# An expert layer's weights used as fp32 instead of as two fp32r halves

## The chip, the cores and the metric

One core of one Trainium2 chip runs the whole kernel in one launch. The metric is device microseconds, the median of several runs. All times come from such runs or from one profiled execution of the kernel before.

## The reference

Three stages follow each other. The change touches the last one alone.

```python
attn = softmax(rmsnorm(q) @ rmsnorm(k).T / 8) @ v          # 4 batches x 12 heads, 448 rows of 64
x = attn as [1792, 768]
# first expert layer: each token goes to its best expert of 8
x[mask] = gate_w[mask, None] * (np.maximum(x[mask] @ w1[e], 0) @ w2[e])
# second expert layer: each expert takes 224 tokens, handed out in order of the highest logit
for idx in np.argsort(-(x @ w_gate).flatten()):
    tok, e = idx // 8, idx % 8
    if assigned[tok] < 0 and counts[e] < 224: assigned[tok] = e; counts[e] += 1
for e in range(8):
    h = np.maximum(x[assigned == e] @ w1[e], 0.0)          # 224x768 @ 768x1024
    out[assigned == e] = h @ w2[e]                         # 224x1024 @ 1024x768
```

All arrays are fp32.

## The kernel before

`moe2` computes the second expert layer. Handing out the tokens is a sequential job: after each phase one more expert is full. The class `Assigner` does it, mostly in short vector instructions (comparisons of bids, lines 1599 to 1960), with small matmuls, transposes and copies on the other engines. Phase 0 is over before `moe2` begins its products; in the path that ran, a compaction follows (line 1913), then phases 1 to 6 (`phase`: `bids`, `count`, `settle`, `put`) and a short `last`. Each ends with `ids` (line 1865), the row numbers of one expert's tokens.

The products of one expert run beside the phases of later ones. For each expert `n` in the order in which they fill up:

- `gather` fetches its 224 token rows in two halves by indirect DMA on the GpSimd queue (L2076); `turn` transposes them (12 transposes, L2084).
- The weights come in 14 pieces on SyncE's queue (L2051): six of w1 (128x1024, 512 KB) and eight of w2 (128x768, 384 KB). They land in a ring of six places (`raws`). `split` makes two fp32r halves of each piece: ScalarE copies the high half (L2066), and VectorE or GpSimd subtracts it for the low half (L2057). The table `ON_V` says which: all six w1 pieces of an expert after the first go to VectorE, all w2 pieces to GpSimd. A fp32 product is then high times high, high times low and low times high.
- The transposed tokens are halved likewise (ScalarE L2088, VectorE L2090).
- First product, 48 steps (8 column blocks `f` by 6 row blocks `k`): `acc` issues three matmuls of 224 columns (L2098 to L2100). `relu` copies on ScalarE (L2123, L2124) and subtracts on GpSimd. When no assignment step is left, `acc2` issues a matmul of 448 and one of 224 columns (L2107, L2108) and `relu2` does a chain on ScalarE and VectorE (L2113 to L2118).
- Second product, 32 steps (2 token halves, 2 column halves, 8 `k`): `gemm2` issues three matmuls of 384 columns (L2135 to L2137). `store` copies out and scatters by indirect DMA (L2142, L2143).

The order on each engine is written out when the program is built. `Pace.work` keeps a clock for each engine with the costs given in the code, such as `work("p", 0.32, t)` for a step of the first product and 0.485 for one of the second; ahead of each step of the experts it emits all assignment steps that would be ready by then. The engines run their queues in order, so a matmul of the assignment that waits for VectorE holds the experts' matmuls behind it on TensorE.

The first weight piece is loaded as soon as expert 0 is known; a memset on GpSimd (behind the gathers on that queue) holds the next ones back until the gathers are issued, and the fourth w1 piece of each later expert likewise (L2047).

Of the kernel before, what the change touches and what calls it, by code (L numbers as in the profile page):

```python
# [1960 lines left out]
def moe2(tc, consts, wt, qkv, x0, asn, w1, w2, y, out):  # L1961
# [8 lines left out]
    with ExitStack() as ctx:  # L1970
# [3 lines left out]
        w1h, w1l, w2h, w2l = wt  # L1974
# [5 lines left out]
        raws = [t[:, FF * i : FF * i + FF] for t in qkv for i in range(3)]  # L1980
        xx = p2.tile([128, KD, 2, CAP], F32R, name="xx")
        xh, xl = xx[:, :, 0, :], xx[:, :, 1, :]
        hh = p2.tile([128, KF, CAP], F32R, name="hh")
        hl = p2.tile([128, KF, CAP], F32R, name="hl")
        zr = x0[0]
        xgs = [p2.tile([CP, YW], F32, name=f"xg{i}") for i in range(2)]
        hrs = [p2.tile([128, CAP], F32, name=f"hr{i}") for i in range(NHR)]

        def product(f):
            return pg2[f % 2][:, : 2 * CAP]  # L1990
# [37 lines left out]
        nload, nsplit = 0, 0  # L2028

        arrival, there, done = {}, {}, {}  # L2030
# [6 lines left out]
        def pump(eng=nc.sync, most=6):  # L2037
            nonlocal nload
            while nload < nsplit + most:
                n, first, k = piece(nload)  # L2040
                if n >= len(regs):
                    break
                if (n, first, k) == (n, True, LATE) and n:

                    if (n, 1) not in fetched:
                        break
                    nc.gpsimd.memset(raws[nload % 6][0:1, 0:1], 0.0)  # L2047
                r, w, wd = raws[nload % 6], w1 if first else w2, FF if first else DM
                clock["d"] = max(clock["d"], clock["p"] + DELAY, choice[n]) + wd * 1.43e-3
                arrival[nload] = clock["d"]  # L2050
                eng.dma_start(out=r[:, :wd], in_=w[bass.ds(regs[n], 1), 128 * k : 128 * (k + 1), :].rearrange("a p f -> p (a f)"))  # L2051
                nload += 1

        def subtract(out, in0, in1, t, width, on_v):

            t = work(*(("v", 0.05 + width * 1.07e-3) if on_v else ("g", width * 2.25e-3)), t)
            (nc.vector if on_v else nc.gpsimd).tensor_tensor(out=out, in0=in0, in1=in1, op=OP.subtract)  # L2057
            return t

        def split(n, first, k):  # L2060
            nonlocal nsplit
            assert piece(nsplit) == (n, first, k) and nload > nsplit
            r = raws[nsplit % 6]
            h, l, wd = (w1h, w1l, FF) if first else (w2h, w2l, DM)
# [3 lines left out]
            nsplit += 1  # L2068
            if nsplit > 1:
                pump()  # L2070
# [31 lines left out]
        def acc2(n, pg, f, k):  # L2102

            fs = slice(128 * f, 128 * f + 128)
            t = max(there[n, True, k], there["x", 0, k // 3], there["x", 1, k // 3])
            done[f] = work("p", 0.285, t)
            nc.tensor.matmul(pg, lhsT=w1h[:, k, fs], rhs=xx[:, k].rearrange("p a c -> p (a c)"), start=k == 0, stop=False)  # L2107
            nc.tensor.matmul(pg[:, :CAP], lhsT=w1l[:, k, fs], rhs=xh[:, k, :], start=False, stop=k == KD - 1)  # L2108

        def relu2(pg, f):  # L2110
            hr = hrs[f % NHR]
            t = work("s", 0.25, max(done[f], there.get(("h", f - NHR), 0.0)))
            nc.scalar.activation(hr, pg[:, CAP:], AF.Copy)  # L2113
            t = work("v", 0.3, t)
            nc.vector.tensor_tensor(out=hr, in0=pg[:, :CAP], in1=hr, op=OP.add)  # L2115
            nc.vector.tensor_scalar(hh[:, f, :], hr, 0.0, None, op0=OP.max)  # L2116
            there["h", f] = work("v", 0.6, t)
            nc.vector.scalar_tensor_tensor(hl[:, f, :], hr, 0.0, hh[:, f, :].bitcast(F32), op0=OP.max, op1=OP.subtract)  # L2118

        def relu(pg, f, on_v=False):  # L2120
            hr = hrs[f % NHR]
            t = work("s", 0.68, max(done[f], there.get(("h", f - NHR), 0.0)))
            nc.scalar.activation(hr, pg, AF.Relu)  # L2123
            nc.scalar.activation(hh[:, f, :], hr, AF.Copy)  # L2124
            there["h", f] = subtract(hl[:, f, :], hr, hh[:, f, :].bitcast(F32), t, CAP, on_v)

        def gemm2(n, h, t):
# [28 lines left out]
        start = nload, nsplit, known, list(regs), dict(asn.__dict__)  # L2156

        def experts(compact):
            nonlocal nload, nsplit, known
            nload, nsplit, known = start[:3]  # L2160
            regs[:] = start[3]
            choice[:] = [0.0]
            fetched.clear()
            asn.__dict__.update(start[4])
            arrival.update((i, 0.0) for i in range(FIRST))
            pace.start(phases(compact), g=2.0, d=3.5)
            ready.update({0: 4.5, 1: 5.5})
            split(0, True, 0)
# [8 lines left out]
            split(0, True, 1)  # L2177
            for n in range(E):
                turns, gathered, turned = [], 0, 0
                splits = iter(range(KD) if n + 1 < E else ())  # L2180
                both = pace.step is None

                def ahead(t):
# [7 lines left out]
                    elif t >= 17:  # L2191
# [8 lines left out]
                        if t % 2 and nload > nsplit and arrival[nsplit] <= clock["p"] + EARLY:  # L2200
                            k = next(splits, None)
                            if k is not None:
                                split(n + 1, True, k)

                for t in range(32):
                    k2 = t // 2 + 2
                    if n and t % 2 == 0 and 2 <= t <= 16:
                        (relu2 if both else relu)(product(t // 2 - 1)[:, : CAP << both], t // 2 - 1)
                    if n == 0 and 7 <= t < 7 + KF:
                        split(0, False, t - 7)  # L2210
                    if t % 2 == 0:
                        if n == 0 and k2 < KD:
                            split(0, True, k2)
                        elif n and k2 < KF:
                            split(n, False, k2)
# [6 lines left out]
                    if t < 16:  # L2222
                        if n:
                            f, a = divmod(t, 2)
                            for k in range(3 * a, 3 * a + 3):
                                (acc2 if both else acc)(n, product(f)[:, : CAP << both], f, k)
# [5 lines left out]
                        elif t < 6 + KF:  # L2232
# [4 lines left out]
                            for i in range(f - 1, f + 1) if f % 2 else ():  # L2237
                                relu(first_product(i), i, i in ON_V[4])
                    else:
                        gemm2(n, (t - 16) // 8, t % 8)  # L2240
                if n + 1 == E:
# [9 lines left out]
                for k in splits:  # L2251
                    split(n + 1, True, k)
                split(n + 1, False, 0)
                split(n + 1, False, 1)
# [13 lines left out]
EARLY = 0.3  # L2268
# [15 lines left out]

ON_V = (0, 1, 3, 5), range(6), (), (), ()


def fused_kernel(tc, q, k, v, g_q, g_k, modality_id, w_gate, bias, w1, w2, w_gate2, w12, w22, out):
    nc = tc.nc
    with ExitStack() as ctx:  # L2290
        cpool = ctx.enter_context(tc.tile_pool(name="cpool", bufs=1))
        dpool = ctx.enter_context(tc.tile_pool(name="dpool", bufs=1, space=bass.MemoryType.DRAM))
        wp1 = ctx.enter_context(tc.tile_pool(name="wp1", bufs=1))
        xp = ctx.enter_context(tc.tile_pool(name="xp", bufs=1))
        xs = dpool.tile([N, DM], F32, name="xs")
# [4 lines left out]
        rp = ctx.enter_context(tc.tile_pool(name="rp", bufs=1))  # L2300
# [42 lines left out]
```

## Time and profile before

| | us |
|---|---|
| median of 3 runs | 1146.68 |
| lowest, highest | 1145.34, 1154.47 |
| the profiled execution | 1148.52 |
| its span, first to last instruction | 1146.5 |
| mean granted TensorE clock in it | 0.932 of full |

The span is what the profile's rows cover; 2.0 us of the profiled execution lie outside it. Attention fills the span to about 350 us, the first expert layer to about 705 us, and `moe2` the rest.

### The profile page before, as it was taken

What the parts mean: (1) busy time and instruction counts of PE and PEld (TensorE: products, weight loads), DVE (VectorE), ACT (ScalarE), POOL (GpSimd) and SP (SyncE); (2) the same over time, 40 slices, a digit from 0 to 9 for tenths busy, and PEclk for the clock granted to TensorE, in tenths of its full rate; (3) what the DMA queues carried; (4) which work ended last, traced back from release to release, by engine and by line L of the source; (5) the groups of instructions that cost most, each with busy time, mean ns of one, the idle gap of its engine ahead of it and who ended that gap; (6) DMA issues with size and microseconds to landing.
All of it is one profiled execution on the core that took longest, in us unless ns stands there. A gap on an engine that the chain in (4) does not pass through costs nothing. (4 is left out here: it accounts for less than half of the span.)

```text
span 1146.5 us, 19734 instructions
## 1 busy us (share of the span) xinstructions
PE 1029.6 (90%) x6480; PEld 823.0 (72%) x6480; DVE 670.0 (58%) x1634; ACT 527.7 (46%) x1139; POOL 384.1 (33%) x330
## 2 busy tenths in 40 slices
PE   7999999999996999999999988588798969889875
PEld 6566555556554888889889876577687869789775
DVE  5777877868857511113212127868888783786670
ACT  3677777677783222224422228342444344355330
POOL 4533344343145110010501010252627162663350
PEclk7999999999998999999999989588797889999988
DMA  6566555555462173466201010515616082675530
GB/s 150 134 155 154 132 142 142 132 138 130 118 190 73 57 263 112 167 235 232 80 30 57 28 49 11 185 61 188 197 40 218 32 250 89 200 235 168 163 108 27
DMA packets 80903, 151.10 MB, mean 132 GB/s; under 512 B 14254, under 2 KB 53422, under 8 KB 80752
## 3 DMA queue, kind: packets, MB, share of 16 engines
q1 hardware_dynamic: 75552, 126.06, 37.8%
q0 software_dynamic: 5200, 23.33, 6.5%
q8 instruction: 58, 0.95, 0.4%
q14 instruction: 93, 0.76, 0.2%
HBM read 110.69 MB, written 17.44 MB: 112 GB/s over the span
## 5 line engine op out<-in xcount | busy, mean ns | idle before, releaser
L205 DVE TENSOR_REDUCE nm<-sp 112x1 f32<-112x448 f32 x192 | 117.9, 619 | 57.3 <-PE sp L204 29.5
L211 ACT ACTIVATE e<-sp,nm 112x448 f32<-112x448 f32 x192 | 121.8, 634 | 54.7 <-DVE nm L205 35.1
L2057 POOL TENSOR_TENSOR w2l<-qkv,w2h 128x768 fp32r<-128x768 f32 x64 | 124.1, 1954 | 59.8 <-ACT w2h L2066 36.6
L219 PE MATMUL tp<-ident,e 112*112 112x112 f32 x768 | 111.8, 269 | 0.6 <-DVE et L222 0.6
L219 PEld LDWEIGHTS tp<-ident,e 112*112 112x112 f32 x768 | 81.7, 135 | 26.1 <-issue 19.0
L232 PE MATMUL op<-et,qkv 112*64 112x448 f32 x384 | 99.4, 565 | 0.0
L225 ACT ACTIVATE et<-tp 112x448 f32<-112x448 f32 x144 | 78.4, 545 | 36.6 <-PE tp L219 35.1
L2135 PE MATMUL bank<-w2h,hh 128*112 128x384 f32 x256 | 91.1, 356 | 0.0
L2137 PE MATMUL bank<-w2h,hl 128*112 128x384 f32 x256 | 86.9, 339 | 0.0
L2136 PE MATMUL bank<-w2l,hh 128*112 128x384 f32 x256 | 86.7, 339 | 0.0
L2107 PE MATMUL bank<-xx,w1h 128*128 128x448 f32 x192 | 67.2, 400 | 21.1 <-DVE hr L2115 21.0
L200 PE MATMUL sp<-bt,at 128*112 128x448 f32 x188 | 85.4, 454 | 0.7 <-DMA bt<-cut 0.6
L908 PE MATMUL po<-w2h,hh 128*128 128x384 f32 x240 | 85.5, 356 | 0.1
L137 POOL TENSOR_TENSOR xn<-qkv,rr 112x512 f32<-112x512 f32 x47 | 48.0, 1053 | 112.2 <-DVE rr L128 112.2
L909 PE MATMUL po<-w2l,hh 128*128 128x384 f32 x240 | 81.5, 339 | 0.5 <-DVEq L837 0.5
L880 PE MATMUL pg<-w1h,xh 128*128 128x512 f32 x180 | 75.0, 417 | 7.1 <-ACTq L1192 5.7
L911 PE MATMUL po<-w2h,hl 128*128 128x384 f32 x240 | 80.2, 339 | 0.0
L984 POOL DMA_INDIRECT y<-yr,ti x11 | 11.5, 1041 | 194.6 <-POOLq L837 165.1
L882 PE MATMUL pg<-w1h,xl 128*128 128x512 f32 x180 | 71.2, 396 | 0.0
L881 PE MATMUL pg<-w1l,xh 128*128 128x512 f32 x180 | 70.8, 393 | 0.0
L2098 PE MATMUL bank<-xx,w1h 128*128 128x224 f32 x192 | 68.4, 356 | 0.0
L200 PEld LDWEIGHTS sp<-bt,at 128*112 128x112 f32 x188 | 33.9, 180 | 47.6 <-issue 31.9
(441 smaller groups left out, 2487.6 us busy)
## 6 DMA issues: line engine op xcount, KB each, us to landing
qkv<-in_moe_w_dram SPq DMA_DIRECT2D x104, 384.0 KB, 4.3
qkv<-in_moe_w_dram SPq DMA_DIRECT2D x48, 512.0 KB, 4.4
raw<-in_moe_w_dram SPq DMA_DIRECT2D x24, 512.0 KB, 5.5
bt<-cut SPq DMA_DIRECT2D x96, 112.0 KB, 2.2
at<-cut SPq DMA_DIRECT2D x96, 112.0 KB, 2.3
qkv<-in_v_dram SPq DMA_DIRECT2D x12, 448.0 KB, 6.6
xs<-xp SPq DMA_DIRECT2D x24, 224.0 KB, 2.9
qkv<-in_k_dram SPq DMA_DIRECT2D x11, 448.0 KB, 4.4
```

The costliest lines, as they stand in the source:

```text
L200: nc.tensor.matmul(sp, lhsT=at[:, h, cs], rhs=bt[:, h, :], start=h == 0, stop=h == 1)
L205: nc.vector.tensor_reduce(out=st["nm"][:, n : n + 1], in_=sp, axis=AX.X, op=OP.max, negate=True)
L211: nc.scalar.activation(e, st.pop(("s", n)), AF.Exp, bias=st["nm"][:, n : n + 1], accum_out=st["sm"][:, n : n + 1])
L219: nc.tensor.transpose(tp[:, kc, :], e[:, kc * CP : (kc + 1) * CP], ident[:CP, :CP])
L232: nc.tensor.matmul(st["op"][h * D : (h + 1) * D, :], lhsT=raws[i // 2][:, 2, 2 * (i % 2) + h, kc * D : (kc + 1) * D], rhs=st["et"][:, h, k ...
L908: nc.tensor.matmul(po[n], lhsT=hh[:, k, :], rhs=w2h[:, kk, cs], start=kk == 0, stop=False)
L909: nc.tensor.matmul(po[n], lhsT=hh[:, k, :], rhs=w2l[:, kk, cs], start=False, stop=False)
L911: nc.tensor.matmul(po[n], lhsT=hl[:, k, :], rhs=w2h[:, kk, cs], start=False, stop=kk == KF - 1)
L2057: (nc.vector if on_v else nc.gpsimd).tensor_tensor(out=out, in0=in0, in1=in1, op=OP.subtract)
L2135: nc.tensor.matmul(po, lhsT=hh[:, k, ts], rhs=w2h[:, k, cs], start=k == 0, stop=False)
L2136: nc.tensor.matmul(po, lhsT=hh[:, k, ts], rhs=w2l[:, k, cs], start=False, stop=False)
L2137: nc.tensor.matmul(po, lhsT=hl[:, k, ts], rhs=w2h[:, k, cs], start=False, stop=k == KF - 1)
```

## The change

In `moe2` the halves disappear. Each product step is one fp32 matmul, `w1s[n % 2]` and `w2s[n % 2]` are two places for all weights of an expert, and the DMAs write into them directly. `raws`, `split`, `subtract`, `acc2`, `relu2`, `ON_V` and the halves of the tokens and of the hidden layer are gone; `relu` is one ScalarE instruction, and `turn` has one copy on ScalarE in place of a copy and a subtraction. A piece may be loaded for expert `n` when the products of expert `n - 2` that read the same place have been issued (`firsts`, `seconds`). The planner's costs change with it. The two pairs of places lie in the 96 KB per partition that held the four halves; the pools are opened in another order so that these can be closed after the first expert layer. Assignment, gathers, transposes and stores stay.

```diff
-            while nload < nsplit + most:
+            while most is None or nload < most:
                 n, first, k = piece(nload)
-                if n >= len(regs):
+                if n >= len(regs) or n > (firsts if first else seconds) + 1:
                     break
-                if (n, first, k) == (n, True, LATE) and n:
+                r = (w1s if first else w2s)[n % 2][:, k, :]
+                if (first, k) == (True, LATE) and n:
...
-                    nc.gpsimd.memset(raws[nload % 6][0:1, 0:1], 0.0)
-                r, w, wd = raws[nload % 6], w1 if first else w2, FF if first else DM
+                    nc.gpsimd.memset(r[0:1, 0:1], 0.0)
+                w, wd = (w1, FF) if first else (w2, DM)
...
-            t = work("s", 0.1 + wd * 8.3e-4, arrival[nsplit])
-            nc.scalar.activation(h[:, k, :], r[:, :wd], AF.Copy)
-            there[n, first, k] = subtract(l[:, k, :], r[:, :wd], h[:, k, :].bitcast(F32), t, wd, k in (ON_V[0 if n == 0 else 1] if first else ON_V[2 if n == 0 else 3]))
...
-            t = work("s", 0.33, t)
-            nc.scalar.activation(xh[dst], px, AF.Copy)
-            there["x", h, i] = work("v", 0.42, t)
-            nc.vector.tensor_tensor(out=xl[dst], in0=px, in1=xh[dst].bitcast(F32), op=OP.subtract)
+            there["x", h, i] = work("s", 0.45, t)
+            nc.scalar.activation(xt[dst], px, AF.Copy)
...
-            done[f] = work("p", 0.32, t)
-            nc.tensor.matmul(pg, lhsT=w1h[:, k, fs], rhs=xh[:, k, :], start=k == 0 and not (shared and f % 2), stop=False, **check)
-            nc.tensor.matmul(pg, lhsT=w1h[:, k, fs], rhs=xl[:, k, :], start=False, stop=False, **check)
-            nc.tensor.matmul(pg, lhsT=w1l[:, k, fs], rhs=xh[:, k, :], start=False, stop=k == KD - 1, **check)
...
+            done[f] = work("p", 0.378, t)
+            nc.tensor.matmul(pg, lhsT=w1s[n % 2][:, k, fs], rhs=xt[:, k, :], start=k == 0 and not (shared and f % 2), stop=k == KD - 1, **check)
+
+        def relu(pg, f):
+            there["h", f] = work("s", 0.38, done[f])
+            nc.scalar.activation(ht[:, f, :], pg, AF.Relu)
...
-                work("p", 0.485, max(there[n, False, k], there["h", k]))
+                work("p", 0.646, max(there[n, False, k], there["h", k]))
                 cs = slice(384 * i, 384 * i + 384)
-                nc.tensor.matmul(po, lhsT=hh[:, k, ts], rhs=w2h[:, k, cs], start=k == 0, stop=False)
-                nc.tensor.matmul(po, lhsT=hh[:, k, ts], rhs=w2l[:, k, cs], start=False, stop=False)
-                nc.tensor.matmul(po, lhsT=hl[:, k, ts], rhs=w2h[:, k, cs], start=False, stop=k == KF - 1)
+                nc.tensor.matmul(po, lhsT=ht[:, k, ts], rhs=w2s[n % 2][:, k, cs], start=k == 0, stop=k == KF - 1)
...
-            work("s", 0.8)
+            work("s", 0.98)
...
-        for r in raws[FIRST:6]:
-            nc.gpsimd.memset(r[0:1, 0:1], 0.0)
+        nc.gpsimd.memset(w1s[0][0:1, FIRST, 0:1], 0.0)
```

## Rows read from the trace of the kernel before

**Rows 1.** The page, first part: busy time, share of the span, instructions.

```profile
PE 1029.6 (90%) x6480; PEld 823.0 (72%) x6480; DVE 670.0 (58%) x1634; ACT 527.7 (46%) x1139; POOL 384.1 (33%) x330
```

**Rows 2.** Busy time by stretch: experts 0 to 4 and 7, first matmul to next expert's.

```profile
core 0: us, PE busy (x) PEld busy (x) DVE busy (x) ACT busy (x) POOL busy (x), PEclk, DMA share, GB/s
...
734.60:801.90 67.30, 56.44 (x371) 50.52 (x370) 51.67 (x141) 24.74 (x46) 28.10 (x22) 0.82 0.43 144
801.90:863.20 61.30, 51.73 (x338) 45.16 (x337) 51.07 (x127) 27.68 (x51) 25.80 (x22) 0.83 0.41 127
863.20:923.40 60.20, 53.47 (x345) 47.30 (x344) 48.99 (x127) 24.31 (x47) 26.09 (x22) 0.83 0.41 128
923.40:973.40 50.00, 40.94 (x270) 40.14 (x269) 28.07 (x48) 20.39 (x38) 24.18 (x21) 0.86 0.51 156
973.40:1013.20 39.80, 34.10 (x206) 32.01 (x205) 28.08 (x35) 18.94 (x32) 19.69 (x14) 1.00 0.63 192
...
1091.70:1133.90 42.20, 35.58 (x194) 33.31 (x192) 19.07 (x25) 9.86 (x20) 16.63 (x10) 0.92 0.20 65
```

**Rows 3.** Groups of VectorE instructions by line and shape, 734.6 to 973.4 us.

```profile
L2057 DVE TENSOR_TENSOR w1l<-qkv,w1h 128x1024 fp32r<-128x1024 f32 x27 | 31.9, 1220 | 2.5 <-ACT w1h L2066 2.4
...
L2090 DVE TENSOR_TENSOR xx<-bank,xx 128x336 fp32r<-128x336 f32 x17 | 8.5, 501 | 17.8 <-ACT xx L2088 17.6
```

**Rows 4.** VectorE in order of time (start, duration), about 815 to 820 us.

```profile
815.24 0.34 DVE L1707 SCALAR_TENSOR_TENSOR g<-rows,bid,tri 128x128 bf16<-128x128 f32 x1
...
817.63 2.55 DVE L1707 SCALAR_TENSOR_TENSOR g<-rows,bid,tri 128x128 bf16<-128x128 f32 x1
```

**Rows 5.** GpSimd in order of time, the same microseconds.

```profile
815.06 1.10 POOL L2143 DMA_INDIRECT out_dram<-x,ids  x1 [0.30 <-ACT hr L2123]
...
818.19 1.83 POOL L2057 TENSOR_TENSOR w2l<-qkv,w2h 128x768 fp32r<-128x768 f32 x1
```

**Rows 6.** VectorE in order of time: milestones of the assignment.

```profile
724.36 0.16 DVE L1865 TENSOR_TENSOR ids<-sum 112x2 int32<-112x2 f32 x1
...
736.25 5.88 DVE L1947 TENSOR_SCALAR g<-i128a,tm 128x128 f32<-128x128 f32 x8
...
743.19 1.06 DVE L1947 TENSOR_SCALAR g<-i128a,tm 128x128 f32<-128x128 f32 x5
...
748.21 0.21 DVE L1615 TENSOR_REDUCE bid<-mn 128x8 f32<-128x64 f32 x1
...
778.46 1.19 DVE L1853 TENSOR_SCALAR g<-i,k 128x112 bf16<-128x112 bf16 x7
...
838.67 0.21 DVE L1615 TENSOR_REDUCE bid<-mn 128x8 f32<-128x64 f32 x1
...
856.10 0.39 DVE L1845 TENSOR_TENSOR place<-u,hid 128x224 bf16<-128x224 f32 x1
...
945.25 0.16 DVE L1865 TENSOR_TENSOR ids<-sum 112x2 int32<-112x2 f32 x1
```

**Rows 7.** TensorE in order of time, matmuls of the three-matmul steps at full clock.

```profile
745.87 0.28 PE L2100 MATMUL bank<-xx,w1l 128*128 128x224 f32 x1
...
746.20 0.28 PE L2100 MATMUL bank<-xx,w1l 128*128 128x224 f32 x1
...
1041.12 0.34 PE L2135 MATMUL bank<-w2h,hh 128*112 128x384 f32 x1
...
1041.64 0.33 PE L2135 MATMUL bank<-w2h,hh 128*112 128x384 f32 x1
```

**Rows 8.** TensorE in order of time: two fp32 products of the attention stage.

```profile
301.28 0.66 PE L259 MATMUL fpt<-rmat,ot 128*112 128x144 f32 x4
```

**Rows 9.** The instructions of line 259: durations min/median/max in ns.

```profile
L259 PEld LDWEIGHTS fpt<-rmat,ot x188: 172/176/179, 47.1 to 350.1; 128*112 128x112 f32 x188
L259 PE MATMUL fpt<-rmat,ot x188: 283/286/378, 47.2 to 350.2; 128*112 128x144 f32 x188
```

**Rows 10.** Who waited for whom, 973.4 to 1091.7 us: total, times, longest.

```profile
PE bank L2107 <- DVE hr L2115: 14.5, 12, 2.9
```

More of the change, by code (lines that the diff above doesn't have):

```diff
@@ L1958, in compact, with moe2 @@
         return t
-def moe2(tc, consts, wt, qkv, x0, asn, w1, w2, y, out):
+def moe2(tc, consts, wt, x0, asn, w1, w2, y, out):
     nc = tc.nc
@@ L1978, in moe2 @@
         asn.bank, asn.counts = lambda: next(turns), lambda: next(turns)
[L1980 to L1984, printed above, removed]
+        xt = p2.tile([128, KD, CAP], F32, name="xtt")
+        ht = p2.tile([128, KF, CAP], F32, name="ht")
         zr = x0[0]
         xgs = [p2.tile([CP, YW], F32, name=f"xg{i}") for i in range(2)]
-        hrs = [p2.tile([128, CAP], F32, name=f"hr{i}") for i in range(NHR)]
         def product(f):
-            return pg2[f % 2][:, : 2 * CAP]
+            return pg2[f % 2][:, :CAP]
         def first_product(f):
@@ L2035, in piece, with pump @@
             return n, k < KD, k if k < KD else k - KD
-        def pump(eng=nc.sync, most=6):
+        def pump(most=None):
             nonlocal nload
-            while nload < nsplit + most:
+            while most is None or nload < most:
                 n, first, k = piece(nload)
-                if n >= len(regs):
+                if n >= len(regs) or n > (firsts if first else seconds) + 1:
                     break
-                if (n, first, k) == (n, True, LATE) and n:
+                r = (w1s if first else w2s)[n % 2][:, k, :]
+                if (first, k) == (True, LATE) and n:
                     if (n, 1) not in fetched:
                         break
-                    nc.gpsimd.memset(raws[nload % 6][0:1, 0:1], 0.0)
-                r, w, wd = raws[nload % 6], w1 if first else w2, FF if first else DM
+                    nc.gpsimd.memset(r[0:1, 0:1], 0.0)
+                w, wd = (w1, FF) if first else (w2, DM)
                 clock["d"] = max(clock["d"], clock["p"] + DELAY, choice[n]) + wd * 1.43e-3
-                arrival[nload] = clock["d"]
-                eng.dma_start(out=r[:, :wd], in_=w[bass.ds(regs[n], 1), 128 * k : 128 * (k + 1), :].rearrange("a p f -> p (a f)"))
+                there[n, first, k] = clock["d"]
+                nc.sync.dma_start(out=r, in_=w[bass.ds(regs[n], 1), 128 * k : 128 * (k + 1), :].rearrange("a p f -> p (a f)"))
                 nload += 1
[L2054 to L2064, printed above, removed]
-            t = work("s", 0.1 + wd * 8.3e-4, arrival[nsplit])
-            nc.scalar.activation(h[:, k, :], r[:, :wd], AF.Copy)
-            there[n, first, k] = subtract(l[:, k, :], r[:, :wd], h[:, k, :].bitcast(F32), t, wd, k in (ON_V[0 if n == 0 else 1] if first else ON_V[2 if n == 0 else 3]))
-            nsplit += 1
-            if nsplit > 1:
-                pump()
         def gather(n, h):
@@ L2096, in acc @@
             t = max(there[n, True, k], there["x", 0, k // 3], there["x", 1, k // 3])
-            done[f] = work("p", 0.32, t)
-            nc.tensor.matmul(pg, lhsT=w1h[:, k, fs], rhs=xh[:, k, :], start=k == 0 and not (shared and f % 2), stop=False, **check)
-            nc.tensor.matmul(pg, lhsT=w1h[:, k, fs], rhs=xl[:, k, :], start=False, stop=False, **check)
-            nc.tensor.matmul(pg, lhsT=w1l[:, k, fs], rhs=xh[:, k, :], start=False, stop=k == KD - 1, **check)
[L2102 to L2125, printed above, removed]
+            done[f] = work("p", 0.378, t)
[3 more added lines that the diff above has]
+            nc.scalar.activation(ht[:, f, :], pg, AF.Relu)
         def gemm2(n, h, t):
@@ L2152, in moe2 @@
             gather(0, h)
-        for r in raws[FIRST:6]:
-            nc.gpsimd.memset(r[0:1, 0:1], 0.0)
+        nc.gpsimd.memset(w1s[0][0:1, FIRST, 0:1], 0.0)
         few = nc.values_load(asn.regs[0:1, E : E + 1], engines=tuple(ALL), min_val=0, max_val=1)
-        start = nload, nsplit, known, list(regs), dict(asn.__dict__)
+        start = nload, known, list(regs), dict(asn.__dict__)
         def experts(compact):
-            nonlocal nload, nsplit, known
-            nload, nsplit, known = start[:3]
-            regs[:] = start[3]
+            nonlocal nload, known, firsts, seconds
+            nload, known = start[:2]
+            firsts, seconds = 0, 0
+            regs[:] = start[2]
             choice[:] = [0.0]
             fetched.clear()
-            asn.__dict__.update(start[4])
-            arrival.update((i, 0.0) for i in range(FIRST))
+            asn.__dict__.update(start[3])
+            there.update(((0, True, k), 0.0) for k in range(FIRST))
             pace.start(phases(compact), g=2.0, d=3.5)
             ready.update({0: 4.5, 1: 5.5})
-            split(0, True, 0)
             pump()
@@ L2199, in ahead @@
                             turned += 1
[L2200 to L2203, printed above, removed]
                 for t in range(32):
-                    k2 = t // 2 + 2
                     if n and t % 2 == 0 and 2 <= t <= 16:
[L2208 to L2215, printed above, removed]
+                        relu(product(t // 2 - 1), t // 2 - 1)
                     if n and t == 3:
@@ L2225, in experts @@
                             for k in range(3 * a, 3 * a + 3):
-                                (acc2 if both else acc)(n, product(f)[:, : CAP << both], f, k)
+                                acc(n, product(f), f, k)
                         elif t < 6:
@@ L2237, in experts @@
                             for i in range(f - 1, f + 1) if f % 2 else ():
-                                relu(first_product(i), i, i in ON_V[4])
+                                relu(first_product(i), i)
+                        if t == 15:
+                            firsts = n + 1
                     else:
                         gemm2(n, (t - 16) // 8, t % 8)
+                seconds = n + 1
                 if n + 1 == E:
@@ L2292, in fused_kernel @@
         dpool = ctx.enter_context(tc.tile_pool(name="dpool", bufs=1, space=bass.MemoryType.DRAM))
-        wp1 = ctx.enter_context(tc.tile_pool(name="wp1", bufs=1))
         xp = ctx.enter_context(tc.tile_pool(name="xp", bufs=1))
+        rp = ctx.enter_context(tc.tile_pool(name="rp", bufs=1))
+        weights = ctx.enter_context(ExitStack())
+        wp1 = weights.enter_context(tc.tile_pool(name="wp1", bufs=1, reuse_waits="tile"))
         xs = dpool.tile([N, DM], F32, name="xs")
@@ L2306, in fused_kernel @@
         rt, e0, slot0 = front(tc, consts, rp, q, k, v, g_q, g_k, modality_id, w_gate, bias, xs, w1, w2, (w1h, w1l), qkv, x0, l2, y)
[L2307 removed]
+        wp2 = weights.enter_context(tc.tile_pool(name="wp2", bufs=1, reuse_waits="tile"))
         w2h = wp2.tile([128, FF // 128, DM], F32R, name="w2h")
@@ L2318, in fused_kernel @@
         asn = moe1(tc, consts, rt, e0, slot0, xs, wt, qkv, x0, w1, w2, w_gate2, y, assigner)
-        moe2(tc, consts, wt, qkv, x0, asn, w12, w22, y, out)
+        weights.close()
+        wp3 = ctx.enter_context(tc.tile_pool(name="wp3", bufs=1, reuse_waits="tile"))
+        w1s = [wp3.tile([128, DM // 128, FF], F32, name=f"w1s{i}") for i in range(2)]
+        w2s = [wp3.tile([128, FF // 128, DM], F32, name=f"w2s{i}") for i in range(2)]
+        moe2(tc, consts, (w1s, w2s), x0, asn, w12, w22, y, out)
 _INS = ["q", "k", "v", "g_q", "g_k", "moe_modality_id", "moe_w_gate", "moe_modality_bias", "moe_w1", "moe_w2", "moe2_w_gate", "moe2_w1", "moe2_w2"]
```

17 lines of the change are left out of this document (3 added, 14 removed).

## The prediction

> **What bounds the kernel now.** I read the page first: TensorE is busy for 90% of the span [rows 1], which would speak against any change that gives it more to do. That share mixes stages, so the next view is busy time by stretch, cut at the first matmul of each expert [rows 2]. It shows two different halves of `moe2`. Experts 0 to 3, while tokens are still handed out, take 67.3, 61.3, 60.2 and 50.0 us, together 238.8, at a granted clock of 0.82 to 0.86; VectorE is busy for 49 to 52 us of each of the first three. Expert 4 takes 39.8 us at full clock, expert 7 takes 42.2, and from 973.4 to 1133.9 this half is 160.5 us; its four stretches are alike, and the first and the last stand in the rows.
>
> How much of it is TensorE's own work? Three matmuls of 224 columns take 0.33 us from start to start (745.87 to 746.20), three of 384 take 0.52 [rows 7]. An expert of the first half therefore needs 48 x 0.33 + 32 x 0.52 = 32.5 us and some 1.4 us for its transposes (an estimate: 12 at up to 0.11 us, the spacing of a weight-load-bound matmul), 33.9 in all. Four make 136. The stretches hold 371 + 338 + 345 + 270 = 1324 matmuls, of which 4 x 252 are the experts'; the other 316 are the assignment's, at most 35 us at 0.11 each, less because the narrow ones run four at a time: I take 24. So of 238.8 us about 78 are neither: waiting, or half clock that follows from waiting.
>
> What it waits for is the assignment on VectorE. The order-of-time view shows why that is slow: the same instruction (L1707) takes 0.34 us at 815.24 and 2.55 us at 817.63 [rows 4], and at that moment GpSimd runs its subtraction for w2 [rows 5]. On top of such stretching VectorE does 27 subtractions of w1 (31.9 us) and 17 for the tokens (8.5 us) between 734.6 and 973.4 [rows 3].
>
> In the second half the stall is another one: the first product waits for the `relu2` chain on VectorE, 14.5 us over experts 4 to 6 as the view of waits has it [rows 10].
>
> **The change part by part.**
>
> *Fp32 products, more TensorE work.* The nearest row is line 259, a fp32 product of 144 columns. Two products leave four records [rows 8], so each is two passes. Four starts lie in 0.66 us, the last of them 0.286 long [rows 9]: (0.66 - 0.286) / 3 = 0.125 us a pass. [...] One expert: 48 x 0.378 + 32 x 0.645 + 1.4 = 18.1 + 20.6 + 1.4 = 40.2 us, 6.3 more than the 33.9 above. [...]
>
> The weight load beside each pass is 0.176 us [rows 9] and is longer than the 0.125 between starts, so it overlaps the pass before. [...]
>
> *Splits, relu and token halves removed.* VectorE loses 31.9 + 8.5 us in the first half, GpSimd loses all its tensor work, and with it goes the stretching. ScalarE loses the high halves; it keeps one copy per relu. None of this is on the path except through the assignment. GpSimd keeps the indirect DMAs. While one ran (815.06 to 816.16), L1707 on VectorE took its 0.34 us at 815.24 [rows 4, 5], no stretch like the 2.55 later, so I cost them at nothing.
>
> [...]
>
> *How long the assignment then takes.* It runs from 724.4 (ids of expert 0) to 945.25 [rows 6]. The compaction, 724.4 to 748.2, contains three w1 subtractions (3.7), four token subtractions (2.0) and eight L1947 in 5.88 us where five alone took 1.06 (4.2 too many): 23.8 - 9.9 = 13.9, so it ends near 738. The least disturbed phase is the fourth: 838.67 to 856.49, in which four token subtractions (2.0) stand; with its seven L1853 (1.2) and some 1.3 for the last matmuls and sums it is 17.8 - 2.0 + 2.5 = 18.3 us, waits for TensorE included. Six phases are 110, and `last` I put at 9: the end is near 857. If each phase waits 2.5 us more for a TensorE that is now fuller, it is 872.
>
> *How much expert work lies ahead of that point in TensorE's queue.* Before, the assignment ended at 945, 0.7 of the way through expert 3's first product: some 3.7 experts at the planner's 30.9 us (48 x 0.32 + 32 x 0.485), 114 planned us. The planner had counted some 32 us of subtractions into VectorE's queue; without them 82 planned us remain, and at its new 38.8 an expert that is 2.1 experts. In 857 - 734.6 = 122 us TensorE needs 2.1 x 40.2 + 24 = 108, so it waits some 14 us in this stage, or spends them at half clock. After it come 5.9 experts at 40.2, less 1.4 because the last has no transposes to do: 857 + 235.8 = 1092.8. The floor, TensorE never waiting, is 734.6 + 8 x 40.2 + 24 - 1.4 = 1078.8.
>
> *Experts 4 to 7.* 4 x 40.2 - 1.4 = 159.4 against 160.5. The relu stall goes and fp32 streaming takes its place: no gain, no loss. What is late next is TensorE itself. The new relu hides behind the other bank's product (six steps, 2.3 us, against about 0.4).
>
> *Loads.* The bytes and the queue are the same: 6.3 MB an expert, at a DMA share of 0.41 to 0.63 [rows 2]. An expert now needs them once in 40 us, and whole experts may be ahead. Three new waits arise on SyncE, a place still read by expert n - 2; behind a waiting DMA stand only later pieces and reads of expert numbers, needed some 40 us later. The held-back first pieces keep their memset. I cost this at nothing; if the cover failed, 6.3 MB would be exposed once, some 19 to 21 us at a full share of the DMA engines (144 / 0.43 to 192 / 0.63 give 335 to 305 GB/s).
>
> *End.* From the last matmul at 1133.9 [rows 2] to the span's end at 1146.5 are 12.6 us, unchanged. So the span becomes 1092.8 + 12.6 = 1105.4, with 2.0 outside it 1107.4 for such an execution; the profiled one was 1.8 above the median of the runs, so 1105.6. I say 1106.
>
> **The rivals.**
>
> *TensorE never waits:* floor 1078.8 + 12.6 + 0.2 = 1092. For it speaks that dense matmuls hold the clock (1.00 in expert 4 [rows 2]); against it, that the assignment alone needs 122 us and the planner puts 108 us of work beside it.
>
> *The handoffs remain:* the 78 lost us are due not to VectorE's load but to queues in order on four engines, each phase handing over between them, and to the half clock that follows. Then they stay, and 4 x 6.3 = 25 us of added streaming come on top: 1146.7 + 25 - 1 = 1171. It decides from the point where less than 25 of the 78 go. Against it: the undisturbed phase takes 18.3 us, waits included, where six of them and `last` took 197.
>
> [...]
>
> [...]
>
> *The change does only half of what it says,* because loads into two places run late: one exposed expert costs 20 us: 1126.
>
> **How the numbers follow.** Forecast (1095 to 1119) 0.62; TensorE never waits 0.12; fuller passes, late assignment or late loads (1119 to 1134) 0.15; a result within 1% of before 0.03; handoffs remain 0.06; exposed loads 0.02. The range 1090 to 1132 takes in the first three nearly whole. One per cent, 11.5 us, is about what a measurement of this kernel can tell from no change. Faster by over 1% is 0.62 + 0.12 + 0.15 = 0.89, within it 0.03, slower 0.08.
>
> **What would show it.** In the profile after: product passes 0.19 and 0.32 us apart; experts 4 to 7 at 40 us each at full clock; L1707 never above 0.5 us; the last `ids` near 857 in place of 945; the last matmul near 1093. The prediction is wrong if phases still take over 25 us with VectorE idle between steps, if the granted clock stays near 0.82 through the first experts, or if TensorE waits for weights from DMA.

## The result, and the profile after

The changed kernel took 1102.76 us (median of 4 runs, 1102.58 to 1104.28), the kernel before 1150.58 beside it (4 runs, 1145.34 to 1155.18): a ratio of 0.959, 95% interval 0.956 to 0.962. The forecast was 1106, the range 1090 to 1132. The profiled execution took 1102.77 us, 1.8 of them outside its span.

First the page of the changed kernel, its first part and the head of the chain that ended last; it answers to [rows 1].

```profile
span 1101.0 us, 18184 instructions
...
PE 1043.8 (95%) x6032; PEld 769.6 (70%) x6032; DVE 468.5 (43%) x1460; ACT 420.9 (38%) x995; POOL 233.5 (21%) x228
...
PE 31%; issue 1%; DVE 1%; DMA 0%; POOL 0%; ACT 0%; DVEq 0%; POOLq 0%; ACTq 0%
```

TensorE is busy for 14 us more than before in a span that is 45 us shorter. Where the time went is seen by stretch, as in [rows 2]: the start of the layer, experts 0 to 4, expert 7.

```profile
core 0: us, PE busy (x) PEld busy (x) DVE busy (x) ACT busy (x) POOL busy (x), PEclk, DMA share, GB/s
734.00:741.70 7.70, 7.70 (x40) 7.70 (x40) 2.23 (x14) 1.35 (x3) 0.00 (x0) 0.50 1.03 395
741.73:797.74 56.01, 55.89 (x316) 37.24 (x316) 40.99 (x186) 10.16 (x27) 5.34 (x7) 0.96 0.66 239
797.74:849.52 51.78, 51.78 (x304) 34.01 (x303) 38.80 (x176) 10.27 (x27) 4.99 (x5) 1.00 0.36 128
849.52:889.91 40.39, 40.39 (x180) 30.86 (x179) 3.39 (x21) 6.40 (x16) 3.91 (x5) 1.00 0.63 218
889.91:929.88 39.97, 39.97 (x173) 30.50 (x172) 0.00 (x0) 6.40 (x16) 3.91 (x5) 1.00 0.54 190
929.88:969.85 39.97, 39.97 (x173) 30.50 (x172) 0.00 (x0) 6.40 (x16) 3.91 (x5) 1.00 0.55 193
1049.78:1088.75 38.97, 38.97 (x161) 29.30 (x159) 0.00 (x0) 5.09 (x13) 1.88 (x2) 1.00 0.06 19
```

From 741.7 on the busy column of PE equals the length of the stretch, but for 0.1 us in expert 0: TensorE does not wait. The granted clock was 0.50 of full from before the first product until 746, which gives expert 0 its 0.96, and then 1.00 to the last matmul. Experts 0 to 3 take 56.0 + 51.8 + 40.4 + 40.0 = 188.2 us where [rows 2] had 238.8: 50.6 saved. Experts 4 to 7 take 929.9 to 1088.75, 158.9 us, where they took 160.5. The first product starts 7.1 us later than before (741.73 against 734.60). 7.1 - 50.6 - 1.6 is 45.1 us earlier, and the last matmul did move by 45.2 (1133.9 to 1088.75).

The milestones of the assignment, which answer to [rows 6], and the instruction of [rows 4] over the whole run (min/median/max in ns):

```profile
727.48 0.16 DVE L1865 TENSOR_TENSOR ids<-sum 112x2 int32<-112x2 f32 x1
...
854.15 0.16 DVE L1865 TENSOR_TENSOR ids<-sum 112x2 int32<-112x2 f32 x1
```

```profile
L1707 DVE SCALAR_TENSOR_TENSOR g<-rows,bid,tri x56: 341/346/352, 685.8 to 838.1; 128x128 bf16<-128x128 f32 x56
```

The assignment ends 91 us earlier. No L1707 is stretched any more. Summed over all VectorE instructions on lines 1540 to 1960 from 724 us on, its own time is 114.3 us where before it was 167.1. The fp32 products, in order of time and by duration:

```profile
894.83 5.46 PE L2076 MATMUL bank<-xtt,w1s 128*128 128x224 f32 x28
...
879.59 4.68 PE L2090 MATMUL bank<-w2s,ht 128*112 128x384 f32 x14
```

```profile
L2076 PEld LDWEIGHTS bank<-xtt,w1s x768: 186/190/337, 741.6 to 1067.6; 128*128 128x128 f32 x192
L2076 PE MATMUL bank<-xtt,w1s x768: 352/353/663, 741.7 to 1067.8; 128*128 128x224 f32 x192
...
L2090 PE MATMUL bank<-w2s,ht x512: 484/486/577, 769.4 to 1088.3; 128*112 128x384 f32 x171
```

768 records are two for each of 8 x 48 products. The spacing is (5.46 - 0.353) / 27 = 0.189 us a pass and (4.68 - 0.486) / 13 = 0.323, so 0.378 and 0.645 us a product, as the forecast had it. That is 0.84 ns a column in both.

### The profile page after: what moved, and what is told of

The parts are those of the page before. It is cut to its first block, busy times and chain, and to the rows that moved or that the text cites. A ratio compares the mean times of both kernels' runs of the same rounds, so it can differ in the third digit from the quotient of the medians.

```text
span 1101.0 us, 18184 instructions
## 1 busy us (share of the span) xinstructions
PE 1043.8 (95%) x6032; PEld 769.6 (70%) x6032; DVE 468.5 (43%) x1460; ACT 420.9 (38%) x995; POOL 233.5 (21%) x228
## 5 line engine op out<-in xcount | busy, mean ns | idle before, releaser
L2090 PE MATMUL bank<-w2s,ht 128*112 128x384 f32 x512 | 176.5, 490 | 0.0
L2076 PE MATMUL bank<-xtt,w1s 128*128 128x224 f32 x768 | 156.5, 358 | 0.0
L2076 PEld LDWEIGHTS bank<-xtt,w1s 128*128 128x128 f32 x768 | 143.4, 191 | 5.2 <-issue 1.2
L211 ACT ACTIVATE e<-sp,nm 112x448 f32<-112x448 f32 x192 | 121.8, 634 | 53.2 <-DVE nm L205 34.1
L2090 PEld LDWEIGHTS bank<-w2s,ht 128*112 128x112 f32 x512 | 86.2, 177 | 59.4 <-issue 1.1
L225 ACT ACTIVATE et<-tp 112x448 f32<-112x448 f32 x144 | 78.4, 546 | 37.8 <-PE tp L219 36.3
L2080 ACT ACTIVATE ht<-bank 128x224 f32<-128x224 f32 x64 | 22.4, 357 | 173.0 <-PE bank L2076 166.7
L2096 POOL DMA_INDIRECT out_dram<-x,ids x16 | 16.9, 1054 | 294.1 <-ACT x L2095 273.3
L896 DVE TENSOR_TENSOR hl<-ph,hh 128x512 fp32r<-128x512 f32 x30 | 20.7, 690 | 80.6 <-ACT hh L893 48.8
```

What stands on the lines that cost most here:

```text
L211: nc.scalar.activation(e, st.pop(("s", n)), AF.Exp, bias=st["nm"][:, n : n + 1], accum_out=st["sm"][:, n : n + 1])
L225: nc.scalar.activation(dst, tp, AF.Copy)
L2076: nc.tensor.matmul(pg, lhsT=w1s[n % 2][:, k, fs], rhs=xt[:, k, :], start=k == 0 and not (shared and f % 2), stop=k == KD - 1, **check)
L2090: nc.tensor.matmul(po, lhsT=ht[:, k, ts], rhs=w2s[n % 2][:, k, cs], start=k == 0, stop=k == KF - 1)
```

## The experiments

The theory that the prediction rests on: VectorE's load, its own subtractions and its stretching by GpSimd, made the assignment long; TensorE, in order, stood behind it; now TensorE is the bound at 40 us an expert. The rival: the half clock and the handing over from queue to queue made the first half slow, whatever VectorE and GpSimd did. Open between the parts of the theory was which of the two loads counts. For each run stand the median, the ratio to the kernel before on the same chip with its 95% interval, the start of the last `ids`, and the length of experts 4 to 7 from first matmul to next first matmul.

| run | us | ratio | last `ids` | experts 4, 5, 6, 7 |
|---|---|---|---|---|
| before | 1150.6 | | 945.2 | 39.8, 39.3, 39.2, 42.2 |
| after | 1102.8 | 0.959 (0.956 to 0.962) | 854.2 | 40.0, 40.0, 40.0, 39.0 |
| b_pool_cut | 1055.0 | 0.916 (0.911 to 0.921) | 884.3 | 33.1, 33.1, 33.1, 32.1 |
| b_vec_cut | 1133.4 | 0.984 (0.978 to 0.991) | 937.0 | 38.2, 40.2, 38.0, 41.0 |
| b_both_cut | 1053.4 | 0.915 (0.910 to 0.920) | 882.4 | 33.1, 33.1, 33.1, 32.1 |
| b_w2_on_vector | 1129.8 | 0.984 (0.979 to 0.988) | 942.5 | 39.9, 35.4, 37.3, 32.1 |
| b_all_vector | 1094.9 | 0.953 (0.949 to 0.958) | 1003.4 | 42.1, 35.4, 39.3, 32.1 |
| a_gpsimd_load | 1124.2 | 0.978 (0.974 to 0.983) | 877.7 | 40.0, 40.0, 40.0, 39.0 |
| a_vector_load | 1122.8 | 0.978 (0.973 to 0.982) | 872.5 | 40.0, 40.0, 40.0, 39.0 |
| hybrid | 1119.2 | 0.972 (0.967 to 0.977) | 853.5 | 43.2, 43.4, 43.5, 39.3 |
| mixed4 | 1075.9 | 0.939 (0.934 to 0.944) | 883.2 | 33.4, 35.0, 37.1, 32.1 |
| mixed3 | 1074.0 | 0.936 (0.932 to 0.940) | 879.2 | 37.2, 34.1, 37.4, 32.1 |

**Which engine's subtractions.** Three cuts in the kernel before. Instructions and their order stay; the two cuts that include GpSimd add one memset of `hl` at the start of `moe2`. The cut on GpSimd:

```diff
-            there[n, first, k] = subtract(l[:, k, :], r[:, :wd], ...)
+            c = 8 if not on_v else wd
+            there[n, first, k] = subtract(l[:, k, :c], r[:, :c], ...)
...
-            there["h", f] = subtract(hl[:, f, :], hr, ...)
+            there["h", f] = subtract(hl[:, f, :8], hr[:, :8], ...)
```

> The kernel before, with every GpSimd subtraction of the second layer (low halves of w2, of expert 0's w1 and of the hidden values) cut to its first 8 columns; instructions, order, waits and TensorE's work stay, so most of those low halves are left out of the result. Theory (the subtractions on GpSimd and VectorE, and GpSimd stretching VectorE, made the assignment long, and TensorE stood behind it in order): VectorE's small instructions in the first experts lose their multi-us stretches, the last assignment (945 us before) ends at 880 to 905, the second half's experts fall from 39.3 us to 34 to 36, and the time is 1065 to 1110 us. Rival (the half clock and the order of the queues made the first half slow, not the load on these two engines): assignment end within 10 us of 945, time within 1% of before (1139 to 1162).

The cut on VectorE leaves `hl` whole and has:

```diff
+            c = 8 if on_v else wd
```

> The kernel before, with VectorE's subtractions of w1's low half cut to the first 8 of 1024 columns (most of that low half is left out of the result); GpSimd's stay whole. Theory: some 6 x 1.2 us of VectorE's time per expert go, but GpSimd still stretches what is left: assignment end 905 to 930, time 1115 to 1140 us, clearly less than the cut on GpSimd gives. If it is only the sum of VectorE's own work that counts and not GpSimd, this run gains most of the two cuts together. Rival (half clock and queue order): within 1% of before.

Both cuts, with `hl` as in the first:

```diff
+            c = 8
```

> The kernel before with both cuts: all low halves of weights, and the hidden values' from GpSimd, made for 8 columns alone (the rest is left out of the result); TensorE's three fp32r products, copies on ScalarE, loads and order stay. Theory: assignment end 850 to 870 as in the changed kernel, then 33.9 us of TensorE per expert and nothing waiting: last matmul near 1036 to 1050, time 1048 to 1065 us, so 40 to 55 us under the changed kernel: 8 x 6.1 us that the fp32 products cost. Rival (the changed kernel's gain comes from loads without a ring or from single products, not from the missing subtractions): time over 1110.

GpSimd's cut took 94 us off, 10 us more than the theory's best; VectorE's took 16, and on top of GpSimd's it gave 1.6, less than the interval. Of the 94 us, 29 lie in experts 4 to 7 (131.4 us in place of 160.5) and the other 65 ahead of them. So GpSimd's subtractions alone account for nearly all that the cuts bring. The end of the assignment moved less: to 884.3 with GpSimd's cut, to 937.0 with VectorE's, where 905 to 930 had been expected, and to 882.4 with both, where 850 to 870 had been expected. The changed kernel's 854.2 is 28 us earlier still. The busy time by stretch of the run with GpSimd cut, experts 0, 1 and 5:

```profile
735.72:783.58 47.86, 47.72 (x371) 42.70 (x370) 36.31 (x141) 24.61 (x46) 9.31 (x22) 0.96 0.58 206
783.58:830.02 46.44, 44.85 (x339) 39.48 (x337) 37.45 (x127) 27.65 (x51) 9.15 (x22) 0.96 0.53 167
942.57:975.66 33.09, 33.09 (x205) 32.05 (x205) 17.47 (x35) 18.54 (x31) 7.01 (x14) 1.00 0.68 233
```

The counts of instructions are those of [rows 2], x371 and x141 for expert 0; but it takes 47.9 us and not 67.3, VectorE is busy for 36.3 and not 51.7, and the granted clock is 0.96 in place of 0.82. The order of the queues is the same, too. So the half clock of before followed from the waits and did not cause them: the rival falls. In the cut on VectorE the stretching is still there, and the assignment's own time is 168.8 us as before. The durations of L1707 in the cut on GpSimd and in the cut on VectorE:

```profile
L1707 DVE SCALAR_TENSOR_TENSOR g<-rows,bid,tri x56: 336/345/367, 683.9 to 859.6; 128x128 bf16<-128x128 f32 x56
```

```profile
L1707 DVE SCALAR_TENSOR_TENSOR g<-rows,bid,tri x56: 335/344/2554, 685.3 to 902.5; 128x128 bf16<-128x128 f32 x56
```

**The load put back into the changed kernel.** Subtractions that nobody waits for, after each relu, once on GpSimd and once, with `nc.vector`, on VectorE:

```diff
             nc.scalar.activation(ht[:, f, :], pg, AF.Relu)
+            nc.gpsimd.tensor_tensor(out=spare[:, :CAP], in0=ht[:, f, :], in1=ht[:, f, :], op=OP.subtract)
+            for i in range(0 if f < 2 else 3 if f == KF - 1 else 1):
+                wide = ht[:, f - 2 : f + 1, :].rearrange("p a c -> p (a c)")
+                nc.gpsimd.tensor_tensor(out=spare, in0=wide, in1=wide, op=OP.subtract)
```

> The changed kernel with idle subtractions on GpSimd, paced by the relus: 8 of 224 and 8 of 672 columns per expert, as many columns as GpSimd had before, less a tenth; nothing waits for their results. Theory (GpSimd stretches VectorE): VectorE's small instructions of the assignment stretch, their sum goes from 114 us to 135 to 165, VectorE's slack of a quarter is used up, the assignment ends at 865 to 890 instead of 854, and the time is 1108 to 1130 us. Rival (GpSimd was only late with its own results, and does nothing to VectorE): sum and end as in the changed kernel, time within 4 us of 1103.

> The same idle subtractions on VectorE in place of GpSimd, in the changed kernel. They take some 8 to 9 us of VectorE per expert. Theory: the assignment's own instructions keep their durations (sum 112 to 118 us), the added work fits mostly into VectorE's idle quarter, assignment end 854 to 865, time 1103 to 1110 us, so less than the load on GpSimd costs. Rival (any elementwise load costs alike): as much as the run with GpSimd.

GpSimd's idle work cost 21 us. The assignment's own VectorE time rose from 114.3 to 137.4 us, and its end moved by 23.6 us, all as the theory expected. GpSimd and VectorE in order of time there:

```profile
778.39 4.47 POOL L2085 TENSOR_TENSOR spare<-ht 128x672 f32<-128x672 f32 x3
```

```profile
778.39 1.40 DVE L1709 TENSOR_SCALAR g<-rows,bid 128x128 bf16<-128x128 f32 x1
...
780.23 1.39 DVE L1707 SCALAR_TENSOR_TENSOR g<-rows,bid,tri 128x128 bf16<-128x128 f32 x1
```

Beside three GpSimd subtractions in a row the two VectorE instructions take 1.40 and 1.39 us, not their 0.28 and 0.34. With the load on VectorE nothing stretches (sum 114.2 us, L1707 at most 352 ns), as expected; but its cost was not 0 to 7 us, it was 20. There the theory was wrong: VectorE's idle quarter (busy for 38.80 of 51.78 us in expert 1 of the changed kernel) was no slack. These are the added instructions between 740 and 860 us, by group:

```profile
L2085 DVE TENSOR_TENSOR spare<-ht 128x672 f32<-128x672 f32 x16 | 13.7, 858 | 0.6
L2082 DVE TENSOR_TENSOR spare<-ht 128x224 f32<-128x224 f32 x16 | 6.2, 389 | 5.2 <-ACT ht L2081 5.1
```

13.7 + 6.2 = 19.9 us of work that the planner does not know moved the end by 18.4 and the time by 20. TensorE waits again in experts 0 and 1 of both runs; here is the run with GpSimd's load, then the one with VectorE's, experts 0 and 1:

```profile
744.15:811.22 67.07, 61.08 (x315) 39.23 (x315) 51.08 (x186) 10.16 (x27) 21.22 (x23) 0.89 0.57 200
811.22:873.10 61.88, 56.38 (x304) 35.94 (x303) 48.81 (x176) 10.28 (x27) 19.32 (x21) 0.97 0.30 107
```

```profile
741.44:805.80 64.36, 59.11 (x315) 38.52 (x315) 50.35 (x202) 10.16 (x27) 5.33 (x7) 0.94 0.60 208
805.80:867.45 61.65, 53.73 (x304) 34.59 (x303) 48.21 (x192) 10.27 (x27) 4.05 (x5) 1.00 0.30 108
```

So in these two runs a microsecond that the planned order does not count cost a microsecond, whether GpSimd stretched it in (23.1 us, cost 21) or VectorE was given it (19.9 us, cost 20). Subtractions that the planner counts cost less: the 27 of 31.9 us [rows 3], cut to 8 columns of some 0.17 us each while the planner went on counting them, gave 16 back, and 1.6 once GpSimd's were gone. That it is the counting that makes the difference is argued, not shown: no run tells the planner of the added load.

**The second half of before.** One condition more in `split` puts w2's low halves on VectorE for the last four experts:

```diff
-... ON_V[2 if n == 0 else 3])
+... ON_V[2 if n == 0 else 3] or (range(KF) if n > 3 else ()))
```

> The kernel before with w2's low halves on VectorE for experts 4 to 7 alone; GpSimd keeps the others, and the hidden values'. The whole computation is done. Theory: the first half and the end of the assignment stay within 10 us of before (945), the last experts go from 39.3 to 34 to 36 us each, time 1130 to 1140: this sets the handoff from GpSimd in the second half apart from its effect on the assignment. Rival (the second half's waits have nothing to do with GpSimd's w2 halves): within 0.5% of before.

The last `ids` stayed (942.5), experts 4 to 7 fell from 160.5 to 144.7 us, and the time by 20. TensorE's wait for the `relu2` chain, the one of [rows 10], fell from 21.0 us over all four experts to 8.0. So more than half of this stall was GpSimd's doing too. The experts did not reach 34 to 36 each (39.9, 35.4, 37.3, 32.1), where the cut on GpSimd has 33.1.

**Can one have the short assignment without the price of fp32?** First, fp32 for experts 0 to 2 and halves, made by ScalarE and VectorE, from expert 3.

```diff
+            if n >= SW:
+                nc.tensor.matmul(pg, lhsT=halves["h1"][:, k, fs], rhs=xh[:, k, :], ...)
...
+                    r = raws[(nload - BASE) % 3][:, : FF if first else DM]
```

> Fp32 products and direct loads for experts 0 to 2, while the assignment needs VectorE; from expert 3 the three fp32r products of halves again, with all weight halves made on ScalarE (copy) and VectorE (subtraction), none on GpSimd; raw weights then pass through three places; the first piece of expert 0 is loaded into another buffer. The whole computation is done. Theory (TensorE is the bound of the changed kernel at 40.0 us per expert, and VectorE and ScalarE are idle once the assignment is over at 854 us): experts 3 to 7 take 33.9 to 35 us each, 25 to 31 us less in all, time 1071 to 1082 us. Rival (the halves bring handoffs back, or the three places are too few for the loads): experts 3 to 7 take 39 us or more, time 1095 to 1115.

Neither holds: experts 3 to 6 take 42.6 to 43.5 us, as slow as the rival said, and the time of 1119 lies above its range as well. By group, ScalarE's copies from the raw places between 889 and 1061 us; then who TensorE waited for, 889 to 1101:

```profile
L2076 ACT ACTIVATE h<-qkv 128x768 fp32r<-128x768 f32 (+1 forms) x56 | 51.1, 932 | 56.6 <-DMA qkv<-in_moe_w_dram 56.5
```

```profile
PE bank L2109 <- ACT h L2076: 12.7, 8, 2.9
PE bank L2111 <- DVE l L2067: 6.5, 10, 0.8
```

ScalarE stands idle for 56.5 us until a load lands, and TensorE waits for ScalarE. What the queue of the loads waited for in the same stretch:

```profile
SPq L2062 <- POOL qkv L2056: 54.4, 4, 13.9
SPq L2062 <- DVE l L2067: 45.3, 38, 2.3
SPq L2062 <- DVE hl L2067: 37.9, 21, 2.2
```

The lower two are VectorE's subtractions that free one of the three places; the first is the memset on GpSimd that holds back the fourth w1 piece of each expert. In the kernel before that memset held the loads back for 4.0 us from 973 to 1134. So both the three places and the memset held the loads back, and no run sets them apart. Second, the kernel before with all its subtractions on VectorE:

```diff
-ON_V = (0, 1, 3, 5), range(6), (), (), ()
+ON_V = range(6), range(6), range(8), range(8), range(8)
...
-        def relu(pg, f, on_v=False):
+        def relu(pg, f, on_v=True):
```

> The kernel before with every subtraction of the second layer on VectorE and none on GpSimd; the whole computation, fp32r halves and all, is done. VectorE then has 6 x 1.22 + 8 x 0.9 + 8 x 0.3 + 4 x 0.5, about 19 us per expert, beside the assignment's 114 us. Theory (it was GpSimd that stretched VectorE's small instructions and handed low halves over late): small instructions keep their 0.2 to 0.5 us, the assignment ends at 885 to 915 us, the last experts take 33.1 to 35 us each, time 1055 to 1080 us, under the changed kernel by 25 to 45. Rival (what counts is the sum of elementwise work, whichever engine has it): VectorE falls behind, TensorE waits, time 1100 to 1150.

Neither holds: 1094.9 lies between the two, and its interval overlaps that of the changed kernel. Nothing is stretched (assignment 112.1 us), but the last `ids` come at 1003.4, not 885 to 915. A likely reason, which no run tests, is that the planner counts 19 us of VectorE per expert and spreads the assignment over them. Third, fp32 where it relieves VectorE most for its price, in the second product of the first experts alone:

```diff
+                if n < SW:
+                    nc.tensor.matmul(po, lhsT=late["ht"][:, k, ts], rhs=w2s[n % 2][:, k, cs], ...)
+                    continue
```

> The kernel before with the second product as the change has it for experts 0 to 3 alone (fp32, w2 straight to two alternating places, hidden values in fp32 with no halves), and three fp32r products of halves in the first product throughout and in the second from expert 4; all halves that are left are made by ScalarE and VectorE, none by GpSimd. The whole computation is done. Theory (GpSimd's subtractions made the kernel before slow; the fp32 products are the price that the change pays, some 6 us per expert, and 3.7 us of it in the second product): assignment end 875 to 900, experts 0 to 3 at 44 to 49 us, experts 4 to 7 at 33 to 35, time 1058 to 1075 us, under both kernels. Rival (without fp32 in the first product too VectorE is too full, as with all its halves on VectorE: 1095): time 1085 to 1105.

The second of the two runs has `SW = 3` in place of `SW = 4`.

> The same with fp32 second products for experts 0 to 2 alone, so one expert less pays for them, but VectorE makes w2's low halves for expert 3 while the assignment may still run. Theory: within 6 us of the run with four experts, better by 3 to 4 us if the assignment is over by then, worse if it is not.

Both do the whole computation and beat both kernels, with intervals that lie wholly under that of the changed kernel. They do not differ from each other by more than their intervals. The run with four fp32 experts came out a microsecond above what was expected of it. Its stretches, experts 0, 1, 4 and 6:

```profile
736.50:786.20 49.70, 49.70 (x332) 36.45 (x331) 37.86 (x131) 17.70 (x33) 3.23 (x4) 0.96 0.63 228
786.20:834.60 48.40, 47.99 (x327) 34.14 (x325) 38.36 (x148) 13.99 (x31) 6.67 (x8) 1.00 0.60 202
...
921.40:954.80 33.40, 33.40 (x206) 32.26 (x205) 23.70 (x42) 17.46 (x29) 5.96 (x5) 1.00 0.63 212
...
989.90:1027.00 37.10, 34.90 (x206) 33.45 (x205) 24.05 (x43) 18.56 (x31) 2.75 (x3) 0.95 0.62 207
```

TensorE works almost without a pause. Experts 5 and 6 lose 2 and 4 us, and the view of waits names the same chain as [rows 10], for 3.8 us over the two, here without GpSimd:

```profile
PE bank L2115 <- DVE hr L2128: 3.8, 2, 2.2
```

## Why the prediction was right

- *Fp32 products.* Forecast 40.2 us an expert, measured 39.97. The overlap of weight loads held: 0.190 us loads beside 0.189 us steps. That leaves nothing of exposed loads, which had a chance of 0.02. The price against the kernel with GpSimd's cut, where TensorE hardly waits, is 1102.76 - 1055.04 = 47.7 us, forecast 8 x 6.3 = 50. No row or run of before shows the 0.378 and 0.645 us a product that the forecast's sum uses: [rows 8, 9] give 0.125 us for a pass of 144 columns, 0.87 ns a column, which in proportion is 0.389 and 0.667 a product and 41.4 an expert. The changed kernel showed 0.378 and 0.645.
- *Length of the assignment.* Forecast end 857, measured 854.2. The phases took 17 to 18 us (`ids` of experts 1 to 6: 760.8, 777.8, 795.8, 812.7, 829.5, 847.6), forecast 18.3.
- *Experts ahead of its end.* Forecast 2.1, measured 2.1 (expert 2 started at 849.5), but the working is wrong. It reads "0.7 of the way through expert 3's first product" as 3.7 experts. A first product is 15.4 of an expert's 30.9 planned us, so that is 3.35 experts, and the same steps then give 1.8 experts and a time of 1116. That 2.1 came out is luck.
- *Why it was long.* Half right. The prediction set VectorE's own subtractions (31.9 + 8.5 us) beside the stretching. The runs give GpSimd's 94 us of the 96 that both cuts bring, and 61 of the 63 by which both move the assignment's end. In the kernel before, all of TensorE's 36 us of waiting from 734.6 to 973.4 are for VectorE, none for a result of GpSimd, and two thirds are for L1853, an instruction that GpSimd stretches (last section):

```profile
PE bank L1858 <- DVE g L1853: 24.0, 10, 7.6
```

The other 28 us of the 91 came with the change alone; both cuts leave the planner's counts as they were. That they come from the new planned order is argued, not tried.

- *TensorE's waiting in this stage.* Here a term was mis-sized: "so it waits some 14 us in this stage, or spends them at half clock" was 0.1 us of waiting in expert 0 and none after, with the half clock gone by 746. In return "734.6" for the first product was 7.1 us too early, and the assignment's work on TensorE, 24 in the forecast, was 347.0 - 318.8 = 28 (741.73 to 1088.75, less 7 x 39.97 + 38.97). What the estimate of 24 leans on stands in the trace of before: three L1949 of 77 columns from 746.38 take 0.50 us, each 0.275, so 0.11 us from start to start as for the 224 columns of [rows 7], with weight loads busy for all of 746 to 747; and four narrow L1670 at 846.52 take 0.29 us together, where the median of one is 0.28. The products of all eight experts took 1.4 less than 8 x 40.2 - 1.4. So -14 + 7 + 4 - 1 is the miss of -4: 1088.75 against 1092.8. The mechanism is that of the rival in which TensorE never waits, which had a chance of 0.12 at 1092 us. That the time lies nearer to the forecast of 1106 is luck: two terms too small made up for most of the one too large.
- *The 7 us.* `ids` of expert 0 came 3.1 us later in this execution. The rest is in order of time on TensorE: all 32 matmuls of the compaction now stand ahead of the first product, at a granted clock of 0.50 (the stretch from 734.0). Before, the product started after six of them. The kernel before, then the changed one:

```profile
733.44 1.43 PE L1949 MATMUL bank<-rows,g 128*128 128x77 f32 x6
734.60 0.53 PE L2098 MATMUL bank<-xx,w1h 128*128 128x224 f32 x1
```

```profile
733.32 1.13 PE L1949 MATMUL bank<-rows,g 128*128 128x77 f32 x4 [0.21 <-DVE g L1947]
...
734.81 1.42 PE L1949 MATMUL bank<-rows,g 128*128 128x77 f32 x6
...
736.59 1.00 PE L1949 MATMUL bank<-rows,g 128*128 128x77 f32 x4
...
737.95 3.98 PE L1949 MATMUL bank<-rows,g 128*128 128x77 f32 x18
741.73 1.78 PE L2076 MATMUL bank<-xtt,w1s 128*128 128x224 f32 x4
```

That the planner puts them first because it no longer counts VectorE's token subtractions there is argued, not tried.

- *Experts 4 to 7.* No gain, as forecast (158.9 for 159.4). But with GpSimd's subtractions cut these experts take 33.1 us each, so the stall that fp32 replaced went with them. That cut leaves most of the low halves out. Of runs that do the whole computation, the best (1074.0) is 29 us under the changed kernel: so much, at least, was still to be had.
- *Loads and tail* at nothing: right. TensorE waits for no DMA, and the tail is 1101.0 - 1088.75 = 12.3 us.

## What to carry to other kernels

When a stage written out in a planned order runs slower than planned, look for instructions whose duration varies: one that takes 0.34 us and 2.55 us pointed at the neighbour engine here, and taking that neighbour's work away was worth more than making the stage's own work less: 94 us against 16, and still 55 when VectorE had to do all of it. A change that removes a disturbance and adds work elsewhere should be split into the two before it is kept: here the removal was worth 94 us (in a run that leaves work out) and the addition cost 48, and using the costly products only where the disturbed engine is short of time gave 1074.

## What the runs showed of the hardware

In these rows GpSimd holds VectorE up, and VectorE GpSimd; by what means no run tests. In the kernel before, GpSimd's subtraction of [rows 5] ends at 818.19 + 1.83 = 820.02. The VectorE instruction of [rows 4] began at 817.63, ahead of that and during the GpSimd subtraction shown here, and ends at 820.18:

```profile
817.42 0.80 POOL L2057 TENSOR_TENSOR hl<-hr,hh 128x224 fp32r<-128x224 f32 x1
```

Later the reverse; VectorE and then GpSimd in order of time:

```profile
860.52 3.49 DVE L2057 TENSOR_TENSOR w1l<-qkv,w1h 128x1024 fp32r<-128x1024 f32 x3
863.92 3.63 DVE L1853 TENSOR_SCALAR g<-i,k 128x112 bf16<-128x112 bf16 x2
```

```profile
862.45 5.05 POOL L2057 TENSOR_TENSOR w2l<-qkv,w2h 128x768 fp32r<-128x768 f32 x2 [5.71 <-DMA qkv<-in_moe_w_dram]
```

VectorE's three large subtractions take 3.49 us, no longer than three elsewhere (1.22 is the median of one). GpSimd's two, 1.83 us each elsewhere, take 5.05: 1.4 more, which is about the time from 862.45 to the last of VectorE's at 864.01. Then it is the turn of two L1853, which take 3.63 us in place of 0.41 and end with GpSimd at 867.5.

The prediction put GpSimd's indirect DMAs at nothing, and they showed no cost to VectorE: with them still in the stage, no L1707 of the changed kernel took over 352 ns. On GpSimd's side the length does vary there. With VectorE idle such a DMA instruction took 0.94 to 0.97 us, beside VectorE's short instructions once 1.43 and once 2.04; why is not tried:

```profile
784.88 1.43 POOL L2096 DMA_INDIRECT out_dram<-x,ids  x1 [20.89 <-DVE g L1709]
786.61 0.94 POOL L2056 DMA_INDIRECT xg<-y,ids  x1 [0.30 <-PE bank L1670]
...
801.60 2.04 POOL L2096 DMA_INDIRECT out_dram<-x,ids  x1 [12.72 <-ACT x L2095]
```
